# Four two-bank PSUM tiles become eight one-bank tiles, and every operation on PSUM takes 512 columns

## The chip, the cores and the metric

One core of one Trainium2 chip. The metric is the device time of one execution in microseconds; where several executions are shown, their median.

## The reference

Three layers over 4 sequences of 768 tokens, in fp32: a linear attention with a decaying state per head, a feed-forward block with a squared relu, and an RMS norm with a gated feed-forward block.

```python
# attention: 8 heads of 64
for t in range(S):
    state = gamma * state + einsum('bhd,bhe->bhde', k[:, :, t], v[:, :, t])
    y[:, :, t] = scale * einsum('bhd,bhde->bhe', q[:, :, t], state)
x = y as [3072, 512]
# first feed-forward, 512 -> 2048 -> 512
h = maximum(x @ w_in, 0);  x = (h * h) @ w_out
# second, 512 -> 1536 -> 512
xn = x / sqrt(mean(x * x) + 1e-6) * rms_g
g = xn @ w_gate;  val = xn @ w_val
out = (g * sigmoid(g) * val) @ w_out2
```

## The kernel before

**Precision.** Each fp32 operand is kept as a high and a low fp32r part (`split`: a cast on ScalarE, a subtraction on VectorE, line 90). A product is three matmuls of 512 columns: high by high, high by low, low by high (`mm3`, lines 173, 174 and 175). `proj` is the four contraction blocks of one output block: twelve matmuls.

**PSUM.** Four tiles, `pa`, `pb`, `ph` and `pr`, each [128, 2, 512] fp32 and so two banks of 2 KB per partition: all eight banks. They live for the whole kernel. A half of one is `ph[:, 0]` or `ph[:, 1]`; some operations read or write a whole tile, 1024 columns.

**Order.** The whole body stands under `manual_schedule`: on each engine the instructions run in the order in which the code issues them. The framework puts in the semaphore waits: an instruction that writes a tile waits for those that read it before, and one that reads waits for those that wrote.

**Stages.** Tokens go in blocks of 512 (six), chunks of 128 for the attention. The times are those of the profiled execution.

- 0 to 258 us: `block1` for blocks 0 and 1, a plain feed-forward, with the attention's chunks visited in between (`scores`, lines 613 to 624, with the mask's multiplication at line 623; `values`; `into_state`). Projections alternate between `ph[:, 0]` and `ph[:, 1]`; the output blocks collect in `pa` and `pb`. `norm1` copies these out.
- 258 to 397 us and 487 to 613 us: `in_phase` for a pair of blocks, 32 projections, again alternating between the two halves of `ph`. Behind each, ScalarE applies relu from PSUM (line 320) and squares in SBUF (line 321). In the second in-phase the weights come through a ring of seven SBUF units that DMA fills, and beside it the weights of the second feed-forward are converted and written back to HBM (`tick`: `magnitude` at line 138 on ScalarE, `convert` on VectorE, then a DMA).
- 397 to 487 us and 613 to 718 us: `out_phase`, the product with `w_out` for a pair of blocks, by a scheme of seven products (P2, P1, P5, P6, P7, P3, P4 in this order) in place of eight. Four units of twelve matmuls for each product; P2, P5 and P3 collect in `pr`, the others in `ph`, and P6, P7, P4 and P3 add to what stands there from the product before. At the end of a product, the tile is copied to SBUF (line 370 for P6, by halves, 372 for P2, P5 and P4) or added to an SBUF tile (line 376 through line 100).
- 718 to 1315 us: three sweeps, one for each pair of blocks, of six calls of `pair` (line 511): gate and value projections by the same seven products, twelve matmuls each, `pr` for P2, P5 and P3, `ph` for P1, P6, P7 and P4. ScalarE copies (525, 530, 535), VectorE adds (line 100), and `act2` makes the gated value: sigmoid on ScalarE (478), the gate's multiplication (480) and the value's (481) on VectorE, and a split. The last `act2` of a pair reads `ph` itself: 478 and 480 its first half, 481 its second. Between P1 and P5 and before P7 stand matmuls of the output product into `pa` and `pb`; what is left of it runs at the end of a sweep (`out2_late`), a block of 36 matmuls into alternating halves of `pr`, each copied out at line 508.

Of the kernel before, what the change touches and what calls it, by code (L numbers as in the profile page):

```python
# [51 lines left out]
def retention_then_two_mlps(  # L52
# [22 lines left out]
    pa, pb, ph, pr = (ps.tile([128, 2, TB], F32, name=n) for n in ("pa", "pb", "ph", "pr"))  # L75
# [23 lines left out]
    def plus(out_, a, b):  # L99
        nc.vector.tensor_tensor(out=out_, in0=a, in1=b, op=ALU.add)  # L100

# [75 lines left out]
    class Operand:  # L177
# [13 lines left out]
        def put(self, o, src, two_banks):  # L191
            if self.whole and not two_banks:
                split(self.t[0][0][:, :, o], self.t[1][0][:, :, o], src, nc.vector)
            elif self.whole:
                h, l = (t[0][:, :, o].rearrange("p (k a) i -> p k a i", k=2) for t in self.t)
                split(h, l, src, nc.vector)
            else:
                for k in range(2):
                    split(self.t[0][k][:, :, o], self.t[1][k][:, :, o], src[:, k], nc.vector)
# [22 lines left out]
    accs = [pa[:, 0], pa[:, 1], pb[:, 0], pb[:, 1]]  # L222
# [9 lines left out]
    def sums(tot):  # L232
        if due:
            tots, sqs = due.pop(0)
            tots.append(tot)
            for i, sq in enumerate(sqs):
                for h in range(2):
                    for c in range(2):
                        n = 2 * c + h
                        nc.tensor.matmul(  # L240
                            tot[c * D:(c + 1) * D, i, h * C:(h + 1) * C], ones, sq[:, n * C:(n + 1) * C],
                            start=True, stop=True,
                        )

    def rsqrt(js, sqs, last=False):
# [6 lines left out]
        nc.vector.tensor_scalar(m, tots[0], 1.0 / DM, EPS, op0=ALU.mult, op1=ALU.add)  # L252
# [13 lines left out]
    def norm1(j):  # L266
        y = [slot("y") for _ in range(2)]
        for i, (eng, src) in enumerate(((nc.scalar, pa), (nc.vector, pb))):
            copy(eng, y[i], src)
            nc.sync.dma_start(ys[j][:, 2 * i:2 * i + 2, :], y[i])  # L270
        yield
        yield
        for i in range(2):
            nc.scalar.activation(y[i], y[i], AF.Square)
            yield
        for a, b in ((y[0][:, 0], y[0][:, 1]), (y[1][:, 0], y[1][:, 1]), (y[0][:, 0], y[1][:, 0])):
            nc.gpsimd.tensor_tensor(out=a, in0=a, in1=b, op=ALU.add)
            yield
        yield
        yield from rsqrt([j], [y[0][:, 0]])  # L280
# [29 lines left out]
    def in_phase(xs, w_of, after, between):  # L310
        for f in range(NF1):
            q, r, i = f // 4, f % 4 // 2, f % 2
            w = w_of(f)
            for t in range(2):
                proj(w, xs[t], ph[:, t])
# [4 lines left out]
                nc.scalar.activation(a, ph[:, t], AF.Relu)  # L320
# [22 lines left out]
    def out_phase(s, pairs, ahead, y_tile, extra):  # L343
# [9 lines left out]
        for n in range(NOUT):  # L353
# [4 lines left out]
            for m in range(2):  # L358
                mc = slice(m * 128, (m + 1) * 128)
                for c in range(2):  # L360
                    mm3(
                        acc[:, m], u[:, c, 0, mc], u[:, c, 1, mc], xh[:, c], xl[:, c],
# [148 lines left out]
    def pair(n, first, second):  # L511
# [13 lines left out]
        nc.scalar.copy(p1, ph)  # L525
        plus(p1, pr, p1)
# [3 lines left out]
        nc.scalar.copy(p5, pr)  # L530
# [4 lines left out]
        nc.scalar.copy(p6, ph)  # L535
# [4 lines left out]
        plus(p5, ph, p5)  # L540
        act2(p5[:, 0], p5[:, 1], U2[f + 1])
        both(P3, pr, False)
        plus(p6, pr, p6)
        act2(p6[:, 0], p6[:, 1], U2[f])
        both(P4, ph, False)
        act2(ph[:, 0], ph[:, 1], u1[1])

    with tc.manual_schedule():
# [64 lines left out]
        def scores(c, banks, early=False):  # L613
# [3 lines left out]
            sc = banks.rearrange("p h (a i) -> p h a i", a=NP)  # L617
            P = slot("Pt").rearrange("p h (a i) -> p h a i", a=NP)
            for p in range(NP):
                for h, b in enumerate(heads):  # L620
                    nc.tensor.matmul(sc[:, h, p, :], k_[b, p, :], qq[b, p, :], start=True, stop=True)
            table = decays if early else tri_sb.unsqueeze(1).unsqueeze(1).to_broadcast([128, 2, NP, C])
            nc.vector.tensor_tensor(out=P, in0=sc, in1=table, op=ALU.mult)
            pt[c] = P

        def into_state(c):
# [3 lines left out]
            kv = pr[:, 1, 2 * C:].rearrange("p (a d) -> p a d", a=NP)  # L630
# [40 lines left out]

        def visit(c, next_banks, with_sums):
            kv = into_state(c)
            if with_sums:
                sums(pr[:, 0:1, 2 * C:])
            values(c, [pr[:, i, :2 * C].rearrange("p (a i) -> p a i", a=2) for i in range(2)])
# [3 lines left out]
        def after_visit(c, x, kv):  # L680
            x.put(columns_of(c), pr[:, :, :2 * C].rearrange("p k (a i) -> p k a i", a=2), True)
# [16 lines left out]
        warm = ph[:PQ, 0, :128]  # L698
# [14 lines left out]
        def early_values(c, bank):  # L713
            values(c, [bank.rearrange("p (a i) -> p a i", a=NP)])
            cur.put(columns_of(c), bank.rearrange("p (a i) -> p a i", a=NP), False)
# [6 lines left out]
        early_values(0, pr[:, 1])  # L722
# [4 lines left out]
        early_values(1, pr[:, 0])  # L727
        scores(3, pb, early=True)
        early_values(2, ph[:, 0])
        early_values(3, ph[:, 1])  # L730
# [39 lines left out]
        def block1(j, x, sink, visit_at, early, late):  # L770
            nonlocal prev, at_chunk
            first_at = 2 if j == 0 else None
            for f in range(NF1):
# [5 lines left out]
                proj(W[("i", f)], x, ph[:, f % 2])  # L779
                s, r = act1(ph[:, f % 2])  # L780
# [141 lines left out]
        while back:  # L922
            if due:
                sums(pa[:, 0:1, :2 * C])
# [29 lines left out]
        def between2(f, t):  # L954
            background()
            if (f, t) == (3, 0):
                sums(pa[:, :, :2 * C])
# [90 lines left out]
        for s in range(NS):  # L1048
# [7 lines left out]
            for p in range(NPR):  # L1056
                def first():
                    if s == 0:
                        split_wp()
                        load_wp(p + 2)  # L1060
                        if p == 0:
                            sums(pa[:, :, :2 * C])
# [25 lines left out]
            out2_late(0, pr[:, 0])  # L1088
            some(4)
            give(NF2 - 1, 1)  # L1090
            store2(2 * s + 1, 0, pr[:, 0])
            for c in range(1, CB):
                l = pr[:, c % 2]
# [74 lines left out]
```

## Time and profile before

| | us |
|---|---|
| three runs | 1326.19, 1320.39, 1319.2 |
| median | 1320.39 |
| profiled execution | 1317.13 |
| its span in the trace | 1315.3 |
| TensorE busy in it | 1179.9 (90%) |
| VectorE busy | 746.1 (57%) |
| ScalarE busy | 590.3 (45%) |

The busy time of TensorE is modelled: matmuls overlap, and the row of one is longer than its step to the next. The time that a stop costs is read from the starts.

### The profile page before, as it was taken

Reading aid. Unit: us, or ns where it says so; the run is one execution under the profiler, and the core shown is the slowest. Engines: PE = TensorE matmul, PEld = TensorE weight load, DVE = VectorE, ACT = ScalarE, POOL = GpSimd, SP = SyncE. Lnnn points to the kernel's source line nnn. Section 1 sums busy time; section 2 is a strip of 40 time slices with the busy share of each in tenths; the row PEclk is TensorE's granted clock in tenths of the full one; section 3 lists DMA queues with packets and bytes.
Section 4 is the critical chain, followed back from the end, with each engine's and each line's share of the span. In section 5 each row is a group of like instructions: output and inputs, shape, how many; then the busy total and the mean of one; then the engine's idle time right before and its main releaser. Section 6 shows DMA issues by size and latency. Waiting matters only on the chain.

```text
span 1315.3 us, 15650 instructions
## 1 busy us (share of the span) xinstructions
PE 1179.9 (90%) x6070; PEld 930.4 (71%) x6070; DVE 746.1 (57%) x990; ACT 590.3 (45%) x997; POOL 46.2 (4%) x39
## 2 busy tenths in 40 slices
PE   7999998888889898688887899999899999899998
PEld 5788887666667576456665677777677777777776
DVE  5775266523235645432666776776576775667740
ACT  5786435444343425444334445443344443444431
POOL 0000211121100000000000000000000000000000
PEclk9999999999999899899999899999999999999999
DMA  9642455665664378863451121122111122111001
GB/s 362 256 161 89 145 186 201 231 224 207 224 240 160 131 242 269 315 227 112 161 180 68 38 84 49 38 71 100 41 56 33 40 88 81 44 54 32 33 0 65
DMA packets 74211, 175.45 MB, mean 133 GB/s; under 512 B 7948, under 2 KB 20632, under 8 KB 73880
## 3 DMA queue, kind: packets, MB, share of 16 engines
q1 hardware_dynamic: 73560, 174.24, 38.2%
q8 instruction: 48, 0.79, 0.2%
q10 hardware_dynamic: 576, 0.20, 0.1%
q14 instruction: 27, 0.22, 0.1%
HBM read 129.31 MB, written 45.10 MB: 133 GB/s over the span
## 4 chain that ended last, share of the span: by engine, by line
PE 57%; DVE 20%; ACT 14%; issue 5%; DMA 4%; SPq 0%; ACTq 0%; DVEq 0%
PE ph L173 11%; PE ph L174 9%; PE ph L175 9%; PE pr L173 5%; PE pr L174 5%; PE pr L175 5%; DVE part L100 3%; DVE t L481 2%; ACT act L320 2%; DVE t L480 2%; DVE act L97 2%; DVE ring L90 2%; PE pa L173 2%; ACT o L93 2%; PE pa L174 2%
## 5 line engine op out<-in xcount | busy, mean ns | idle before, releaser
L173 PE MATMUL ph<-xop,ring 128*128 128x512 f32 x288 | 116.2, 404 | 25.5 <-DVE t L481 20.9
L173 PE MATMUL ph<-xh,w_i 128*128 128x512 f32 x256 | 104.1, 407 | 30.1 <-ACT act L320 21.6
L174 PE MATMUL ph<-xop,ring 128*128 128x512 f32 x288 | 114.6, 398 | 0.0
L175 PE MATMUL ph<-xop,ring 128*128 128x512 f32 x288 | 114.5, 398 | 0.0
L174 PE MATMUL ph<-xl,w_i 128*128 128x512 f32 x256 | 100.0, 391 | 0.0
L175 PE MATMUL ph<-xh,w_i 128*128 128x512 f32 x256 | 99.8, 390 | 0.0
L173 PE MATMUL pr<-xop,ring 128*128 128x512 f32 x216 | 86.4, 400 | 8.0 <-DVE part L100 6.6
L173 PEld LDWEIGHTS ph<-xop,ring 128*128 128x128 f32 x288 | 55.4, 192 | 43.4 <-DVE t L481 27.2
L174 PE MATMUL pr<-xop,ring 128*128 128x512 f32 x216 | 85.5, 396 | 0.0
L175 PE MATMUL pr<-xop,ring 128*128 128x512 f32 x216 | 85.5, 396 | 0.0
L173 PEld LDWEIGHTS ph<-xh,w_i 128*128 128x128 f32 x256 | 48.0, 187 | 52.5 <-ACT act L320 31.8
L320 ACT ACTIVATE act<-ph 128x512 f32<-128x512 f32 x64 | 38.1, 595 | 104.7 <-PE ph L175 104.7
L90 DVE TENSOR_TENSOR o<-act,o 128x1024 fp32r<-128x1024 f32 x38 | 45.9, 1223 | 62.6 <-ACT o L93 62.6
L173 PE MATMUL ph<-xh,ring 128*128 128x512 f32 x128 | 54.2, 424 | 27.8 <-ACT act L320 26.7
L90 DVE TENSOR_TENSOR ring<-q,ring 128x512 fp32r<-128x512 f32 x90 | 57.4, 686 | 30.6 <-ACT ring L93 30.6
L478 ACT ACTIVATE t<-part 128x512 f32<-128x512 f32 x54 | 34.1, 632 | 79.7 <-DVE part L100 79.7
L93 ACT CAST o<-act 128x1024 fp32r<-128x1024 f32 x38 | 39.1, 1047 | 63.5 <-DVE act L97 60.6
L175 PEld LDWEIGHTS ph<-xop,ring 128*128 128x128 f32 x288 | 55.5, 193 | 12.0
L174 PEld LDWEIGHTS ph<-xop,ring 128*128 128x128 f32 x288 | 55.4, 192 | 11.3
L100 DVE TENSOR_TENSOR part<-pr,part 128x1024 f32<-128x1024 f32 x37 | 45.2, 1220 | 26.7 <-ACT part L525 26.5
L173 PE MATMUL pr<-wp,u 128*128 128x512 f32 x132 | 52.3, 396 | 5.1 <-ACT o L508 5.1
L173 PEld LDWEIGHTS ph<-xh,ring 128*128 128x128 f32 x128 | 24.4, 190 | 45.3 <-ACT act L320 39.3
(230 smaller groups left out, 2785.9 us busy)
## 6 DMA issues: line engine op xcount, KB each, us to landing
ring<-uo SPq DMA_DIRECT2D x56, 512.0 KB, 3.3
q<-wq SPq DMA_DIRECT2D x72, 256.0 KB, 3.2
raw<-w1i SPq DMA_DIRECT2D x16, 512.0 KB, 7.4
raw<-w1o SPq DMA_DIRECT2D x16, 512.0 KB, 6.9
uo<-made SPq DMA_DIRECT2D x16, 512.0 KB, 2.9
wi<-w_i SPq DMA_DIRECT2D x16, 512.0 KB, 5.8
ring<-wi SPq DMA_DIRECT2D x16, 512.0 KB, 4.3
uo<-w_o SPq DMA_DIRECT2D x24, 256.0 KB, 5.1
```

What stands on the lines that cost most here:

```text
L90: eng.tensor_tensor(out=dst_l, in0=src, in1=dst_h.bitcast(F32), op=ALU.subtract)
L93: nc.scalar.copy(dst_h, src)
L97: nc.vector.tensor_tensor(out=out_, in0=a, in1=b, op=ALU.subtract)
L100: nc.vector.tensor_tensor(out=out_, in0=a, in1=b, op=ALU.add)
L173: nc.tensor.matmul(acc, ah, bh, start=start, stop=False, **more)
L174: nc.tensor.matmul(acc, ah, bl, start=False, stop=False, **more)
L175: nc.tensor.matmul(acc, al, bh, start=False, stop=stop, **more)
L320: nc.scalar.activation(a, ph[:, t], AF.Relu)
L478: nc.scalar.activation(t, g, AF.Sigmoid)
L480: nc.vector.tensor_tensor(out=t, in0=g, in1=t, op=ALU.mult)
L481: nc.vector.tensor_tensor(out=t, in0=v, in1=t, op=ALU.mult)
```

## The change

Each of `pa`, `pb`, `ph` and `pr` becomes a list of two [128, 512] tiles, one bank each. Whatever read or wrote a whole tile becomes two instructions of 512 columns, the first bank ahead of the second: the copies (`take`), the adds (`add`), the mask's multiplication in `scores`, the splits in `put`, the first step of `rsqrt`. In `norm1` each tile is copied by both engines, ScalarE its first bank and VectorE its second, in place of one engine for each tile. The rest changes only how a bank is named. VectorE's instructions become 100 more, ScalarE's 74; TensorE's stay as many as they were. The kernel after has other line numbers: its rows name the matmuls of `mm3` as lines 181 to 183 and the multiplications of `act2` as 482 and 483.

```diff
-    pa, pb, ph, pr = (ps.tile([128, 2, TB], F32, name=n) for n in ("pa", "pb", "ph", "pr"))
+    pa, pb, ph, pr = ([ps.tile([128, TB], F32, name=f"{n}{i}") for i in range(2)] for n in ("pa", "pb", "ph", "pr"))
...
+    def take(dst, acc):
+        for m in range(2):
+            nc.scalar.copy(dst[:, m], acc[m])
+
+    def add(dst, acc):
+        for m in range(2):
+            plus(dst[:, m], acc[m], dst[:, m])
...
-        nc.vector.tensor_scalar(m, tots[0], 1.0 / DM, EPS, op0=ALU.mult, op1=ALU.add)
+        for i in range(n):
+            nc.vector.tensor_scalar(m[:, i], tots[0][i], 1.0 / DM, EPS, op0=ALU.mult, op1=ALU.add)
...
-        for i, (eng, src) in enumerate(((nc.scalar, pa), (nc.vector, pb))):
-            copy(eng, y[i], src)
+        for i, src in enumerate((pa, pb)):
+            for m, eng in enumerate((nc.scalar, nc.vector)):
+                copy(eng, y[i][:, m], src[m])
...
             for t in range(2):
-                proj(w, xs[t], ph[:, t])
+                proj(w, xs[t], ph[t])
...
-                nc.scalar.activation(a, ph[:, t], AF.Relu)
+                nc.scalar.activation(a, ph[t], AF.Relu)
...
-                if k == P6:
-                    a = get(0, 1)
-                    for m in range(2):
-                        nc.scalar.copy(a[:, m], acc[:, m])
-                elif k in (P2, P5, P4):
-                    nc.scalar.copy(get(*{P2: (0, 0), P5: (1, 1), P4: (1, 0)}[k]), acc)
+                if k in (P2, P5, P6, P4):
+                    take(get(*{P2: (0, 0), P5: (1, 1), P6: (0, 1), P4: (1, 0)}[k]), acc)
                 else:
                     a = {P1: (0, 0), P7: (1, 1), P3: (0, 1)}[k]
-                    t = y[a[0]][a[1]]
-                    plus(t, acc, t)
+                    add(y[a[0]][a[1]], acc)
                     store(*a)
...
-                product(acc[:, m], k, m, start)
+                product(acc[m], k, m, start)
...
-        nc.scalar.copy(p1, ph)
-        plus(p1, pr, p1)
+        take(p1, ph)
+        add(p1, pr)
...
-        nc.scalar.copy(p5, pr)
+        take(p5, pr)
...
-        nc.scalar.copy(p6, ph)
+        take(p6, ph)
...
-        plus(p5, ph, p5)
+        add(p5, ph)
...
-        plus(p6, pr, p6)
+        add(p6, pr)
...
-        act2(ph[:, 0], ph[:, 1], u1[1])
+        act2(ph[0], ph[1], u1[1])
...
-            nc.vector.tensor_tensor(out=P, in0=sc, in1=table, op=ALU.mult)
+            for h in range(2):
+                table = decays[:, h] if early else tri_sb.unsqueeze(1).to_broadcast([128, NP, C])
+                nc.vector.tensor_tensor(out=P[:, h], in0=sc[h], in1=table, op=ALU.mult)
...
-            out2_late(0, pr[:, 0])
+            out2_late(0, pr[0])
...
-                l = pr[:, c % 2]
+                l = pr[c % 2]
```

Three places in the engines' order. In the names, a number behind a name counts tiles: `ring_3297` and `ring_3352` are the same unit of weights; `ph_153` and `ph_154` are the two banks of `ph` after the change, `pr_155` and `pr_156` those of `pr`. A wait names the engine or DMA queue whose semaphore it reads.

TensorE, second in-phase, two projections in a row; before:

```order
L173 MATMUL ph<-xh,ring_3297 128x512 [waits DMAHW3_49,Activation_49]
L174 MATMUL ph<-xl,ring_3297 128x512
L175 MATMUL ph<-xh,ring_3297 128x512
...
L173 MATMUL ph<-xh,ring_3297 128x512 [waits Activation_49]
L174 MATMUL ph<-xl,ring_3297 128x512
```

and after:

```order
L181 MATMUL ph_153<-xh,ring_3352 128x512 [waits DMAHW3_49,Activation_49]
L182 MATMUL ph_153<-xl,ring_3352 128x512
L183 MATMUL ph_153<-xh,ring_3352 128x512
...
L181 MATMUL ph_154<-xh,ring_3352 128x512 [waits Activation_49]
L182 MATMUL ph_154<-xl,ring_3352 128x512
```

Nothing moved. The wait for ScalarE stands at the same instructions; the tile that it protects is `ph` before, and one bank of it after.

TensorE, P1 of a pair in the sweeps, its first half and the start of its second; before:

```order
L173 MATMUL ph<-xop,ring_3297 128x512 [waits DVE_49]
L174 MATMUL ph<-xop,ring_3297 128x512
L175 MATMUL ph<-xop,ring_3297 128x512
L173 MATMUL ph<-xop,ring_3297 128x512
L174 MATMUL ph<-xop,ring_3297 128x512
L175 MATMUL ph<-xop,ring_3297 128x512
L173 MATMUL ph<-xop,ring_3297 128x512
```

and after:

```order
L181 MATMUL ph_153<-xop,ring_3352 128x512 [waits DVE_49]
L182 MATMUL ph_153<-xop,ring_3352 128x512
L183 MATMUL ph_153<-xop,ring_3352 128x512
L181 MATMUL ph_153<-xop,ring_3352 128x512
L182 MATMUL ph_153<-xop,ring_3352 128x512
L183 MATMUL ph_153<-xop,ring_3352 128x512
L181 MATMUL ph_154<-xop,ring_3352 128x512 [waits DVE_49]
```

One wait for VectorE has become two, one for each bank, six matmuls apart.

VectorE, the end of a pair: the adds of P7 and P3, the three gated values; before:

```order
L100 TENSOR_TENSOR part_4820<-ph,part_4820 128x1024 [waits PE_49]
L480 TENSOR_TENSOR t<-part_4820,t 128x512 [waits Activation_49]
L481 TENSOR_TENSOR t<-part_4820,t 128x512 [waits DVE_49]
L100 TENSOR_TENSOR part_4886<-pr,part_4886 128x1024 [waits PE_49]
L90 TENSOR_TENSOR u_5107<-t,u_5107 128x512 [waits Activation_49]
L480 TENSOR_TENSOR t<-part_4886,t 128x512 [waits Activation_49]
L481 TENSOR_TENSOR t<-part_4886,t 128x512 [waits DVE_49]
L90 TENSOR_TENSOR u_5107<-t,u_5107 128x512 [waits Activation_49]
L480 TENSOR_TENSOR t<-ph,t 128x512 [waits Activation_49]
L481 TENSOR_TENSOR t<-ph,t 128x512 [waits DVE_49]
```

and after:

```order
L100 TENSOR_TENSOR part_4885<-ph_153,part_4885 128x512 [waits PE_49]
L100 TENSOR_TENSOR part_4885<-ph_154,part_4885 128x512 [waits PE_49]
L482 TENSOR_TENSOR t<-part_4885,t 128x512 [waits Activation_49]
L483 TENSOR_TENSOR t<-part_4885,t 128x512 [waits DVE_49]
L100 TENSOR_TENSOR part_4952<-pr_155,part_4952 128x512 [waits PE_49]
L100 TENSOR_TENSOR part_4952<-pr_156,part_4952 128x512 [waits PE_49]
L90 TENSOR_TENSOR u_5176<-t,u_5176 128x512 [waits Activation_49]
L482 TENSOR_TENSOR t<-part_4952,t 128x512 [waits Activation_49]
L483 TENSOR_TENSOR t<-part_4952,t 128x512 [waits DVE_49]
L90 TENSOR_TENSOR u_5176<-t,u_5176 128x512 [waits Activation_49]
L482 TENSOR_TENSOR t<-ph_153,t 128x512 [waits Activation_49]
L483 TENSOR_TENSOR t<-ph_154,t 128x512 [waits DVE_49,PE_49]
```

Each add of two banks has become two instructions with a wait on TensorE of their own, and the last multiplication has a wait on TensorE for its bank.

## Rows read from the trace of the kernel before

**Rows 1.** What TensorE waited for, whole span: total us, times, longest us.

```profile
PE ph L173 <- ACT act L320: 48.3, 54, 6.7
PE ph L173 <- DVE t L481: 20.9, 14, 1.9
...
PE pr L173 <- DVE part L100: 6.6, 3, 2.4
PE pr L173 <- ACT o L508: 6.6, 9, 1.0
PE ph L173 <- DVE Pt L623: 5.2, 4, 2.6
...
PE ph L173 <- ACT y L370: 4.0, 1, 4.0
...
PE ph L173 <- ACT y L372: 1.1, 1, 1.1
```

**Rows 2.** The same view, the first in-phase alone (258 to 397 us).

```profile
PE ph L173 <- ACT act L320: 21.6, 24, 3.0
```

**Rows 3.** The same view, the second in-phase alone (486 to 613 us).

```profile
PE ph L173 <- ACT act L320: 26.7, 30, 6.7
```

**Rows 4.** Timeline, TensorE, second in-phase: start, duration, instruction, idle before and releaser.

```profile
502.51 0.50 PE L173 MATMUL ph<-xh,ring 128*128 128x512 f32 x1 [0.69 <-ACT act L320]
502.85 0.40 PE L174 MATMUL ph<-xl,ring 128*128 128x512 f32 x1
503.09 0.39 PE L175 MATMUL ph<-xh,ring 128*128 128x512 f32 x1
```

**Rows 5.** Windows: length, busy us of engines, granted clock, DMA share, GB/s.

```profile
258.00:397.00 139.00, 117.37 (x819) 87.67 (x817) 41.44 (x57) 60.52 (x110) 21.17 (x16) 1.00 0.63 220
490.00:580.00 90.00, 69.39 (x284) 50.02 (x282) 45.82 (x67) 47.26 (x75) 0.00 (x0) 0.96 0.82 285
530.00:540.00 10.00, 3.33 (x12) 2.42 (x11) 2.11 (x4) 2.46 (x4) 0.00 (x0) 0.73 0.93 365
580.00:613.00 33.00, 26.94 (x108) 19.77 (x109) 1.23 (x1) 11.91 (x19) 0.00 (x0) 1.00 0.33 112
```

**Rows 6.** Timeline, all engines, around TensorE's longest stop.

```profile
537.17 0.66 ACT L138 ACTIVATE f<-raw 128x512 f32<-128x512 f32 x1 [7.88 <-DMA wq<-f]
...
538.96 0.63 PE L174 MATMUL ph<-xl,ring 128*128 128x512 f32 x1
...
539.38 0.63 PE L175 MATMUL ph<-xh,ring 128*128 128x512 f32 x1
```

**Rows 7.** Groups by form: count, busy us, mean ns, idle before and releaser.

```profile
L100 DVE TENSOR_TENSOR part<-pr,part 128x1024 f32<-128x1024 f32 x37 | 45.2, 1220 | 26.7 <-ACT part L525 26.5 <-PE pr L175 0.2
...
L525 ACT COPY part<-ph 128x1024 f32<-128x1024 f32 x18 | 18.3, 1015 | 25.0 <-PE ph L175 25.0
...
L370 ACT COPY y<-ph 128x512 f32<-128x512 f32 x2 | 1.1, 584 | 0.0
```

**Rows 8.** Timeline, VectorE, a pair of the second sweep.

```profile
1015.41 1.29 DVE L90 TENSOR_TENSOR ring<-q,ring 128x512 fp32r<-128x512 f32 x2 [1.24 <-ACT ring L93]
...
1022.00 1.23 DVE L100 TENSOR_TENSOR part<-ph,part 128x1024 f32<-128x1024 f32 x1
1023.99 0.69 DVE L480 TENSOR_TENSOR t<-part,t 128x512 f32<-128x512 f32 x1 [0.76 <-ACT t L478]
...
1025.32 1.22 DVE L100 TENSOR_TENSOR part<-pr,part 128x1024 f32<-128x1024 f32 x1
...
1027.30 0.69 DVE L480 TENSOR_TENSOR t<-part,t 128x512 f32<-128x512 f32 x1 [0.16 <-ACT t L478]
...
1030.02 0.68 DVE L480 TENSOR_TENSOR t<-ph,t 128x512 f32<-128x512 f32 x1
1030.73 0.69 DVE L481 TENSOR_TENSOR t<-ph,t 128x512 f32<-128x512 f32 x1
```

**Rows 9.** Timeline, TensorE, P1 of the pair that follows.

```profile
1031.47 0.50 PE L173 MATMUL ph<-xop,ring 128*128 128x512 f32 x1 [1.35 <-DVE t L481]
```

More of the change, by code (lines that the diff above doesn't have):

```diff
@@ L189, in __getitem__, with put @@
             ]
[L191 to L195, printed above, removed]
+        def put(self, o, banks):
+            n = KC // len(banks)
+            for k, src in enumerate(banks):
+                a = slice(n * k, n * k + n) if self.whole else slice(0, n)
+                h, l = (t[0 if self.whole else k][:, a, o] for t in self.t)
                 split(h, l, src, nc.vector)
-            else:
-                for k in range(2):
-                    split(self.t[0][k][:, :, o], self.t[1][k][:, :, o], src[:, k], nc.vector)
     def proj(w, x, h):
@@ L616, in scores @@
             qq, k_, _, _ = chunk[c]
-            sc = banks.rearrange("p h (a i) -> p h a i", a=NP)
+            sc = [b.rearrange("p (a i) -> p a i", a=NP) for b in banks]
             P = slot("Pt").rearrange("p h (a i) -> p h a i", a=NP)
@@ L620, in scores @@
                 for h, b in enumerate(heads):
-                    nc.tensor.matmul(sc[:, h, p, :], k_[b, p, :], qq[b, p, :], start=True, stop=True)
-            table = decays if early else tri_sb.unsqueeze(1).unsqueeze(1).to_broadcast([128, 2, NP, C])
-            nc.vector.tensor_tensor(out=P, in0=sc, in1=table, op=ALU.mult)
+                    nc.tensor.matmul(sc[h][:, p, :], k_[b, p, :], qq[b, p, :], start=True, stop=True)
+            for h in range(2):
+                table = decays[:, h] if early else tri_sb.unsqueeze(1).to_broadcast([128, NP, C])
+                nc.vector.tensor_tensor(out=P[:, h], in0=sc[h], in1=table, op=ALU.mult)
             pt[c] = P
@@ L670, in columns_of, with halves @@
             return slice((c % B) * C, (c % B + 1) * C)
+        def halves():
+            return [b[:, :2 * C].rearrange("p (a i) -> p a i", a=2) for b in pr]
         def visit(c, next_banks, with_sums):
@@ L674, in visit @@
             if with_sums:
-                sums(pr[:, 0:1, 2 * C:])
-            values(c, [pr[:, i, :2 * C].rearrange("p (a i) -> p a i", a=2) for i in range(2)])
+                sums([pr[0][:, 2 * C:]])
+            values(c, halves())
             scores(c + 1, next_banks)
@@ L680, in after_visit @@
         def after_visit(c, x, kv):
-            x.put(columns_of(c), pr[:, :, :2 * C].rearrange("p k (a i) -> p k a i", a=2), True)
+            x.put(columns_of(c), halves())
             take_state(c, kv)
@@ L714, in early_values @@
             values(c, [bank.rearrange("p (a i) -> p a i", a=NP)])
-            cur.put(columns_of(c), bank.rearrange("p (a i) -> p a i", a=NP), False)
+            cur.put(columns_of(c), [bank.rearrange("p (a i) -> p a i", a=NP)])
         scores(0, pa, early=True)
@@ L956, in between2 @@
             if (f, t) == (3, 0):
-                sums(pa[:, :, :2 * C])
+                sums([b[:, :2 * C] for b in pa])
             if 1 <= f <= 11:
@@ L1061, in first @@
                         if p == 0:
-                            sums(pa[:, :, :2 * C])
+                            sums([b[:, :2 * C] for b in pa])
                             background()
```

26 lines of the change are left out of this document (13 added, 13 removed).

## The prediction

> **What bounds the kernel now.** I read the list of what TensorE waits for first: the matmuls are a fixed series, and whatever stops them lengthens the kernel unless something later was waiting anyway. Its largest entry is one kind of stop, 48.3 us in 54 waits of a projection for the relu of line 320; the next are 20.9 us in 14 waits for the second multiplication of line 481, and 6.6 us each for the adds of line 100 and the copies of line 508 [rows 1]. All are waits to write a PSUM tile that ScalarE or VectorE still reads. The same list by stage puts 21.6 us of the relu's in the first in-phase (258 to 397 us) [rows 2] and 26.7 us in the second (487 to 613 us) [rows 3].
>
> Then the timeline of one such stop, for its price. Matmuls start 0.23 us apart (502.85 and 503.09); behind the stop, which shows 0.69 us idle, the first one lasts 0.50 and the next starts 0.34 later [rows 4]. With 0.39 busy in a usual row against 0.23 from start to start, a stop costs its idle time, plus 0.16, plus 0.11: **idle + 0.27 us**. The reader should see that the stop comes although the projection writes the other half of ph than the one that relu reads: the wait belongs to the tile, not to the bank.
>
> Third, the windows, for what else is near its limit there. The DMA engines are 0.63 busy in the first in-phase, 0.82 in 490 to 580 us, and 0.93 in the ten microseconds in which TensorE stood longest [rows 5]. That stop, the 6.7 of the second in-phase [rows 3], began at ScalarE, which had stood 7.88 us for a transfer, and behind it matmuls start 0.42 us apart (538.96, 539.38), at a granted clock of 0.73 in that window: for part of it the clock was at the lower of its two levels, 1.2 GHz [rows 5, 6].
>
> **The change, part by part.** No matmul, transfer or arithmetic is added or moved. Each engine keeps its order. Two things differ: 174 instructions over two banks become two each (100 on VectorE, 74 on ScalarE), and waits attach to a bank.
>
> *What a split costs.* A 128x1024 add takes 1220 ns, and a 128x512 instruction on VectorE 0.69 us [rows 7, 8]; a 1024 copy takes 1015 ns and a 512 one 584 [rows 7]. Two queued 512s on VectorE span 1.29 us together (1015.41) [rows 8] against 1.22. So a split costs 0.06 to 0.07 us where the two queue behind each other, and at most 2 x 0.69 - 1.22 = 0.16 or 2 x 0.584 - 1.015 = 0.15 where nothing overlaps; 174 x 0.16 = 28 us if all stood on the path. I take the low end, and charge it inside the chains below, since adjacent instructions of one engine overlap in every row of this kind. On the side of the gain, the reader who waits for both halves gets the first half sooner, and the part that must follow the last matmul shrinks from 1.22 to 0.69, or 1.02 to 0.58.
>
> A rule speaks against this. The Trainium skill, Advanced Engine Details and Errata (TRN2 Errata, The Read-Write Bubble), says that memory accesses are not pipelined from one instruction to the next and advises large tiles, even several PSUM banks in one instruction. Its page Perfetto Trace Analysis (Optimizing Scalar/DVE Operations) puts the overhead on PSUM at about 125 ns for VectorE and 51 for ScalarE: an estimate of 100 x 0.125 + 74 x 0.051 = 16 us of engine time, which would be 16 us of span only if no split were hidden. The same section adds that instructions which are not saturating their engine but hold up others may gain by being broken up.
>
> *In-phase 1.* A projection (12 matmuls, 2.72 us) now waits for the relu of the one before the last. The relu has a whole projection to finish in, and every stop seen but one is under 2.72 us. That one, 3.0 us [rows 2], keeps 0.3. Available: 21.6 + 24 x 0.27 = 28.1; I take **27.5**. What could be late next is DMA: 0.63 x 139 us of transfer work in 111.5 us is a share of 0.79, below the 0.93 seen.
>
> *In-phase 2.* Available are 26.7 + 30 x 0.27 = 34.8 us. But from 490 to 580 the transfers weigh: 0.82 x 90 = 74 us of DMA work, which at the highest share seen, 0.93, needs 79 us. So of that stretch 11 us can go, against 23 if TensorE set its length (284 matmuls x 0.23 = 65 us and some waits), and nothing if 0.82 is all that DMA does on a mean. Behind 580 us nine projections follow (108 matmuls) at a DMA share of 0.33 [rows 5], each with the usual stop of 0.69 + 0.27 = 0.96: 8.6. I take 11 + 8.6 = **19.6**, ends 8.6 and 32.
>
> *Out phases.* The wait for line 372 (1.1 + 0.27) goes, because bank 0 is copied while bank 1 is still accumulated: 1.4. The 4.0 us for line 370 [rows 1] stays in large part, since ScalarE was late there for reasons of its own queue; I take 1.0, and 1.0 more for half of the matmuls at the lower clock behind it. **3.4**, ends 0 and 7.5.
>
> *Pairs.* P1 of the next pair waits 1.35 us for line 481, which reads ph's second half; with 0.27 that is 1.62 [rows 8, 9]. With banks, P1's first six matmuls wait only for line 480, and the second six, 1.36 us later, for line 481. Line 480 started 0.71 earlier (1030.02 against 1030.73). To lose the stop wholly it must come another 0.91 earlier. It does so by the chain ahead of it. An add started at 1022.00 and line 480 behind it at 1023.99: the sigmoid between them waited for the add of both banks and needs only that of bank 0, a gain of 1.22 - 0.69 = 0.53. The next add at 1025.32 leads to line 480 at 1027.30, 1.98 later [rows 8]; here two adds and a subtraction stand ahead on VectorE, three steps of 0.60 (1.29 - 0.69) or 1.81 with what is between them, a gain of 0.17. A copy whose first bank is read 1.36 us ahead of the last matmul leaves 1.02 - 0.58 = 0.4 to its followers. Together 0.53 + 0.17 + 0.4 = 1.1 against 0.91: it goes with only **0.2 us to spare**. I take it whole for the ten pairs of sweeps 2 and 3 (16.2). The four of sweep 1 stand for 20.9 - 13.5 = 7.4 of idle; with 4 x 0.27, less 0.3 each that I leave, 7.3. Behind two of these four, the longest of them (1.9), fifteen matmuls in all start 0.42 apart as in rows 6, 0.2 us lost on each: 3.0, and five more, 1.0, behind one of the waits of 2.4 below [rows 1]. The nine waits for the copy of line 508 go, since the banks alternate: 6.6 + 9 x 0.27 = 9.0. The three waits for line 100 (6.6 in all, the longest 2.4) [rows 1], each a two-bank copy and a two-bank add in series, become a one-bank copy and add that start six matmuls sooner: the two longest go, 2 x (2.36 + 0.27) = 5.2, and of the third, at the start of the sweeps, 1.2 of its 1.8: 6.4. Sum 16.2 + 7.3 + 4.0 + 9.0 + 6.4 = **42.9**, ends 19 (no stop at line 481 gained) and 46.
>
> *Start.* Four waits for line 623 [rows 1], each 0.53 sooner: **2.1**.
>
> Sum: 27.5 + 19.6 + 3.4 + 42.9 + 2.1 = 95.5. The profiled execution took 1317.13 us, so 1221.6; the median of the runs was 3.3 above that execution, which gives 1224.9, say **1225 us**.
>
> **The rivals.** *DMA is the bound of the second in-phase already.* For it: the long stop there comes from a transfer. Against: 0.93 was reached. If the share cannot rise above its mean of 0.82, the 11 us are lost: 1236.
>
> *Line 480 comes no sooner.* VectorE's chain takes the place of the wait: 0.2 us of margin is thin, and each split adds 0.06 on it. If 14 stops keep 1.0 us each, 1239; with the first rival, 1250.
>
> *The change doesn't release what it says.* Then a wait is still for both halves, and the time stays at about 1320. Against it: the rows of the new order name the bank in each tile, and the last multiplication has a wait on TensorE of its own for its bank.
>
> *Slower.* Every split pays its full 0.16 us on the path, in chains where VectorE or ScalarE is the last: 28 us, and the chains were long before; 1348 if no wait is given back. It decides as soon as the waits given back are under 28 us; the first in-phase alone holds that, where no instruction at all is split. The page of the Trainium skill (Perfetto Trace Analysis, Optimizing Scalar/DVE Operations) would make it 16 us, 1336.
>
> **How the numbers follow.** The forecast 0.58 (1207 to 1231: all of 32 in the second in-phase, or the out phases and pairs short by a few); DMA 0.14; VectorE's chain, alone or with DMA, 0.20; nothing released 0.04; slower 0.04. The range 1205 to 1248 takes in the first three and the cost ends named, up to both rivals together less 2 us. A measurement can tell 0.5% from no change, 6.6 us: faster 0.93, same 0.03, slower 0.04.
>
> **What would show it.** In the profile after: no wait of a projection for the relu in 258 to 370 us, and a stage some 27 us shorter; in the second in-phase some waits for the relu left, each behind a ScalarE instruction that stood for a transfer, and a DMA share near 0.9; the lines that were 480 and 481 start sooner than before, and P1 shows no wait, or one under 0.3 us; the banks of line 508 alternate without a stop; two 512 adds 0.60 us apart. Wrong would make it: stops of 1 us left at P1 (the chain), waits for the relu with no transfer behind them (not released), or pairs that last over 26 us each.

## The result, and the profile after

The kernel after takes 1218.95 us (median of 4 runs, 1216.87 to 1221.62) against 1319.8 before: a ratio of 0.9235, 95% interval 0.919 to 0.9279. The profiled execution took 1216.87 us, 100.3 us less than the one of before; its span is 1215.0.

The engines' busy time (part 1 of the page): TensorE is at 95% in place of 90%, with less busy time in all: before, more rows were long (behind a stop, or at the lower clock), and a row behind a stop doesn't overlap with the one ahead of it.

```profile
PE 1155.6 (95%) x6070; PEld 934.2 (77%) x6070; DVE 743.0 (61%) x1090; ACT 593.7 (49%) x1071; POOL 44.4 (4%) x39
```

What TensorE waited for, whole span, as in [rows 1] (us in total, times, longest):

```profile
PE ph L181 <- ACT act L327: 10.0, 2, 8.3
PE ph L182 <- DVE o L90: 8.1, 14, 1.0
PE ph L181 <- DVE part L100: 5.8, 1, 5.8
PE ph L181 <- DVE Pt L626: 5.0, 4, 2.3
...
PE ph L181 <- ACT y L104: 3.5, 1, 3.5
...
PE pr L181 <- DVE part L100: 1.3, 1, 1.3
...
PE ph L181 <- DVE t L482: 0.2, 1, 0.2
```

The relu, line 320 before and 327 now, fell from 48.3 us in 54 waits to 10.0 in two. Line 481 (now 483) is gone from the list, and the gate's multiplication ahead of it, now 482, holds P1 once, for 0.2 us. The copies of line 508 are gone. The adds of line 100, for which a product in `pr` waited, are 1.3 in place of 6.6. The mask's multiplication, 5.2 before at line 623, is 5.0 at line 626. One wait has grown: near the start of the sweeps `ph` waits 5.8 us for line 100, where before it was 4.5.

The windows of both in-phases and of the sweeps (length, busy us of TensorE, its weight loads, VectorE, ScalarE and GpSimd, granted clock, DMA share, GB/s), the counterpart of [rows 5]:

```profile
260.00:371.00 111.00, 110.38 (x819) 89.46 (x817) 40.05 (x70) 60.58 (x118) 20.41 (x16) 1.00 0.79 275
460.00:534.00 74.00, 63.98 (x284) 51.81 (x283) 45.57 (x68) 46.66 (x74) 0.00 (x0) 0.95 0.95 348
500.00:510.00 10.00, 7.23 (x25) 5.86 (x26) 5.06 (x9) 6.80 (x11) 0.00 (x0) 0.69 0.97 364
...
716.00:1186.00 470.00, 469.92 (x2066) 386.80 (x2065) 337.81 (x509) 216.85 (x375) 0.00 (x0) 1.00 0.17 56
```

TensorE stands still for 0.6 us in the first in-phase and for 0.1 in the 470 us of the sweeps from 716 on. In the second in-phase the DMA engines are at 0.95 for 74 us.

Where the 100 us went, by aligning the two traces at the same matmul at each stage's border:

| stage | before, us | after, us | gained | predicted |
|---|---|---|---|---|
| 0 to 257.5 of before | 257.6 | 259.5 | -1.9 | 2.1 |
| in-phase 1 | 141.5 | 111.8 | 29.7 | 27.5 |
| out phase 1 | 88.7 | 86.4 | 2.3 | 3.4, both out phases |
| in-phase 2 | 126.0 | 101.3 | 24.7 | 19.6 |
| out phase 2 | 104.5 | 103.7 | 0.8 | in the 3.4 above |
| sweeps | 593.2 | 548.5 | 44.7 | 42.9 |

### The profile page after: what moved, and what is told of

It is laid out like the page before. It is cut to its first block, busy times and chain, and to the rows that moved or that the text cites. A ratio compares the mean times of both kernels' runs of the same rounds, so it can differ in the third digit from the quotient of the medians.

```text
span 1215.0 us, 15870 instructions
## 1 busy us (share of the span) xinstructions
PE 1155.6 (95%) x6070; PEld 934.2 (77%) x6070; DVE 743.0 (61%) x1090; ACT 593.7 (49%) x1071; POOL 44.4 (4%) x39
## 4 chain that ended last, share of the span: by engine, by line
PE 77%; DVE 10%; ACT 7%; issue 3%; DMA 3%; SPq 0%; ACTq 0%; DVEq 0%
PE ph L181 13%; PE ph L182 12%; PE ph L183 12%; PE pr L181 7%; PE pr L182 7%; PE pr L183 7%; DVE act L97 2%; PE pa L181 2%; PE pa L182 2%; PE pa L183 2%; PE pb L181 2%; PE pb L183 2%; PE pb L182 2%; ACT o L93 2%; DMA wq<-f 1%
## 5 line engine op out<-in xcount | busy, mean ns | idle before, releaser
L181 PE MATMUL ph<-xop,ring 128*128 128x512 f32 x288 | 113.5, 394 | 6.0 <-DVE part L100 5.8
L182 PE MATMUL ph<-xop,ring 128*128 128x512 f32 x288 | 112.6, 391 | 0.0
L183 PE MATMUL ph<-xop,ring 128*128 128x512 f32 x288 | 112.6, 391 | 0.0
L183 PE MATMUL ph<-xh,w_i 128*128 128x512 f32 x256 | 100.3, 392 | 0.0
L181 PE MATMUL pr<-xop,ring 128*128 128x512 f32 x216 | 85.0, 393 | 1.4 <-DVE part L100 1.3
L182 PE MATMUL pr<-xop,ring 128*128 128x512 f32 x216 | 84.8, 393 | 0.0
L183 PE MATMUL pr<-xop,ring 128*128 128x512 f32 x216 | 84.6, 392 | 0.0
L181 PEld LDWEIGHTS ph<-xop,ring 128*128 128x128 f32 x288 | 54.4, 189 | 20.1 <-DVE part L100 6.2
L183 PEld LDWEIGHTS ph<-xop,ring 128*128 128x128 f32 x288 | 54.4, 189 | 11.4
L182 PEld LDWEIGHTS ph<-xop,ring 128*128 128x128 f32 x288 | 54.4, 189 | 11.1
L181 PEld LDWEIGHTS ph<-xh,w_i 128*128 128x128 f32 x256 | 48.4, 189 | 18.4 <-DVE Pt L626 6.7
L181 PE MATMUL ph<-xh,ring 128*128 128x512 f32 x128 | 51.0, 398 | 10.0 <-ACT act L327 10.0
L146 ACT ACTIVATE f<-raw 128x512 f32<-128x512 f32 x68 | 45.4, 669 | 29.9 <-DMA wq<-f 16.0
L183 PEld LDWEIGHTS ph<-xh,w_i 128*128 128x128 f32 x256 | 48.4, 189 | 10.7 <-DVE w_i L90 0.4
L182 PEld LDWEIGHTS ph<-xl,w_i 128*128 128x128 f32 x256 | 48.5, 189 | 10.3 <-DVE xl L90 0.5
```

Source lines behind the costliest of these rows:

```text
L146: nc.scalar.activation(sizes[i], loads[i].bitcast(F32)[:, :, 1], AF.Prelu, scale=REBIAS, alpha=NEGATIVE)
L181: nc.tensor.matmul(acc, ah, bh, start=start, stop=False, **more)
L182: nc.tensor.matmul(acc, ah, bl, start=False, stop=False, **more)
L183: nc.tensor.matmul(acc, al, bh, start=False, stop=stop, **more)
```

## The experiments

The first four keep one part of the change, or do one part alone; e1 in an expectation is the first of them. Gains of a stage are read, as in the table, by aligning the traces at the same matmul. The kernel of before was run beside each series of experiments, with medians of 1320.7 to 1322.0 us against the 1319.8 above, so totals that differ by 2 us between series say little.

### The splits without the banks

```diff
-    pa, pb, ph, pr = ([ps.tile([128, TB], F32, name=f"{n}{i}") for i in range(2)] for n in ("pa", "pb", "ph", "pr"))
+    def pair_of(n):
+        t = ps.tile([128, 2, TB], F32, name=n)
+        return [t[:, i] for i in range(2)]
+    pa, pb, ph, pr = (pair_of(n) for n in ("pa", "pb", "ph", "pr"))
```

> The four tiles are two banks each again, but every operation on PSUM takes 512 columns as in the kernel after: the splits without the freed waits. Theory (the gain comes from waits by bank, a split costs 0.06 to 0.07 us where it is queued): the time of the kernel before plus 0 to 8 us, 1318 to 1328 us, with the relu's wait still near 48 us in 54 waits. Rival (the gain comes from the shorter operations): well under 1300 us. Rival (each split pays 0.16 us on the path): 1348 us.

Measured: 1315.38 us, ratio 0.9953 (0.9935 to 0.9972). Half of a percent faster, 3 us below the range that was expected, so neither 28 us slower nor more than 6 of the 100 us. The list of waits (in this kernel line 333 is the relu, 489 the value's multiplication, 516 the copy out, 106 the add):

```profile
PE ph L187 <- ACT act L333: 51.6, 54, 7.3
PE ph L187 <- DVE t L489: 11.2, 14, 1.2
...
PE pr L187 <- ACT o L516: 5.8, 8, 0.7
```

The 54 waits for the relu stay, and so does the copy out. What falls is P1's wait, from 20.9 to 11.2 us in the same 14 places. One of its rows in the second sweep (start, duration, instruction, idle before it), and from the next pair the adds of P7 and the sigmoid behind the first of them:

```profile
1006.20 0.50 PE L187 MATMUL ph<-xop,ring 128*128 128x512 f32 x1 [0.64 <-DVE t L489]
...
1022.89 1.29 DVE L106 TENSOR_TENSOR part<-ph,part 128x512 f32<-128x512 f32 x2
...
1023.68 0.64 ACT L486 ACTIVATE t<-part 128x512 f32<-128x512 f32 x1 [2.05 <-DVE part L106]
```

1.35 has become 0.64: 0.71 us a pair from the splits alone. The sigmoid of `p5`'s first half starts at 1023.68, while the second of the two adds still runs: in SBUF it waits only for the half that it reads. That is the size of the 0.53 + 0.17 = 0.70 of the prediction's chain. The sweeps gain 14.0 us by alignment, and in-phase 1 loses 7.0, in-phase 2 1.7: in the first, ScalarE's wait for the low part of the visits' operand, which VectorE works out from `pr`, is 17.0 us in 8 places against 7.4 in 4. In the kernel with the same splits and `pr` in one-bank tiles (the second of the next section) this wait is not in the list and that stage takes 142.6 us, 1.1 more than before: so it is the two-bank `pr` through which the halves hold each other up there.

### One tile at a time

In `pair_of`, one-bank tiles for the one name and views of a two-bank tile for the others:

```diff
     def pair_of(n):
+        if n == "ph":
+            return [ps.tile([128, TB], F32, name=f"{n}{i}") for i in range(2)]
         t = ps.tile([128, 2, TB], F32, name=n)
```

> Only ph becomes two one-bank tiles; pa, pb and pr keep two banks, operations take 512 columns. Theory: the relu's waits and those of P1 for line 481 go, 29.7 and 24.7 us in the in-phases and most of the 24 us of P1, while the 9.0 us for line 508 and 5 us for line 100, both in pr, stay: 1232 to 1242 us. If P1's chain needs the early add of P3 in pr too, its stops come back in part: up to 1250 us.

Measured: 1236.62 us, ratio 0.9364 (0.9332 to 0.9396).

```profile
PE ph L187 <- ACT act L333: 10.4, 3, 8.4
...
PE pr L187 <- ACT o L516: 5.8, 8, 0.7
...
PE pr L187 <- DVE part L106: 4.7, 3, 1.9
```

The relu's waits are where they are after the change, in-phase 1 gains 28.3 us and in-phase 2 24.1. The waits in `pr` stay: 5.8 us in 8 for the copy out and 4.7 in 3 for the adds, against 1.3 in one after the change. With 0.27 each that is 12 of the 18 us that separate this kernel from the whole change; by alignment 14 of the 18 are in the sweeps.

The same with `pr` in the place of `ph`:

> Only pr becomes two one-bank tiles, the complement: theory, the waits for line 508 (9.0 us) and line 100 (about 5) go, and the splits' cost of e1 is paid: 1300 to 1312 us; the gains of this and of ph alone add up to that of the whole change within some 8 us. If pa and pb matter, the sum falls short by more.

Measured: 1293.91 us, ratio 0.9798 (0.9771 to 0.9825), some 6 us better than the lower end of what was expected, since I had charged the splits a cost that they do not have on balance.

```profile
PE ph L187 <- ACT act L333: 48.8, 54, 6.7
...
PE pr L187 <- DVE part L106: 4.1, 3, 1.4
```

48.8 us of relu stay, and the copy out is gone. Of the adds' waits 4.1 us are left, and with `ph` alone 4.7, against 1.3 after the whole change: these need both tiles. Gains against the kernel of before: 84.7 for `ph`, 27.4 for `pr`; both hold the 5.9 of the splits, so 106 together against 101 for the whole. They add up within 5 us, which leaves nothing for `pa` and `pb`; a kernel with `ph` and `pr` alone wasn't run.

### The freed wait alone, in one stage

```diff
-                proj(w, xs[t], ph[:, t])
+                proj(w, xs[t], halves[t])
...
-                nc.scalar.activation(a, ph[:, t], AF.Relu)
+                nc.scalar.activation(a, halves[t], AF.Relu)
...
-        in_phase(xs2, w_of2, after2, between2)
+        in_phase(xs2, w_of2, after2, between2, [ph[:, 0], pr[:, 0]])
```

> The kernel before, with one difference: in the second in-phase the projections alternate between the first half of ph and the first half of pr, two tiles, in place of the two halves of ph. No split, no other tile. Theory (the stop is a wait for a tile): that stage loses 23 to 26 us and nothing else changes, 1294 to 1298 us. Rival (the gain in that stage needs something else of the change): 1320 us.

Measured: 1297.88 us, ratio 0.9824 (0.9789 to 0.9858). The stage is 22.8 us shorter by alignment, with no instruction split and no tile changed. Its list of waits in that stage:

```profile
PE pr L173 <- ACT act L320: 9.0, 2, 8.3
PE ph L173 <- ACT act L320: 1.7, 1, 1.7
```

Thirty waits have become three, and one of 8.3 us is new. The kernel after has that one too, and of the same length. The third is the out phase's first write to `pr`, 0.7 us. So the stop behind the relu is the wait for a tile, and the long stop that is left doesn't come from the two halves being one tile.

### What is left in the second in-phase

In the kernel after, ScalarE's queue around the longest stop:

```profile
501.57 0.66 ACT L146 ACTIVATE f<-raw 128x512 f32<-128x512 f32 x1 [10.51 <-DMA wq<-f]
...
502.77 0.29 PEld L181 LDWEIGHTS ph<-xh,ring 128*128 128x128 f32 x1 [8.75 <-ACT act L327]
```

The conversion of line 146 stood 10.5 us for a store of an earlier one, and the relu stands behind it on ScalarE. Four kernels ask why.

```diff
-        if i < len(stream):
+        if i < len(stream) and not 7 * NQ <= i < 7 * NQ + NF1:
             nc.sync.dma_start(ring[i % 7].bitcast(F32), stream[i])
```

> The kernel after without the sixteen 512 KB loads of the ring in the second in-phase: its projections use what stands in the ring, so that this part of the result is not computed. Theory (after the change DMA is the bound of that stage): the stops of 8.3 and 1.7 us there and the slow clock behind them go, the stage falls from 101 to 89 to 92 us, 1206 to 1210 us in all. Rival (a shortage of buffers, not of transfer time): within 3 us of the kernel after, 1219.

Measured: 1214.14 us, ratio 0.9192 (0.917 to 0.9215), between the theory and its rival. The stage takes 98.9 us, and not the 89 to 92 that were expected. The windows say why (columns as above):

```profile
475.00:490.00 15.00, 15.00 (x79) 12.15 (x78) 11.23 (x16) 9.10 (x16) 0.00 (x0) 1.00 0.62 212
490.00:500.00 10.00, 3.84 (x17) 2.91 (x16) 0.84 (x3) 1.51 (x4) 0.00 (x0) 0.93 0.98 363
510.00:534.00 24.00, 23.54 (x104) 19.18 (x103) 17.10 (x25) 17.28 (x27) 0.00 (x0) 1.00 0.76 240
```

On a mean the transfers have room, 0.62 and 0.76 of the DMA engines' time on both sides, and the stop of 6.2 us is there all the same, in a stretch of ten microseconds at 0.98. Over the 74 us from 460 to 534 the share fell from 0.95 to 0.82, and the stage gained 2.4 us. That the sum of the transfers was the bound, as the prediction had it, falls; what is left to explain is the stretch of ten microseconds.

> The same omission in the kernel before (that part of the result is not computed either). Theory (there the relu's waits are the bound, and DMA only in one stop): at most the stop of 6.7 us and the slow clock behind it go, 1311 to 1316 us. If DMA had set that stage before already, 10 us or more: under 1310.

Measured: 1318.7 us, ratio 0.9984 (0.9965 to 1.0003); the stage gains 1.0 us, less than expected. Its longest stop is 5.2 us, in the place of the 6.7. The kernel of before is not bound by the sum of its transfers either.

```diff
-        cf = rctx.enter_context(tc.tile_pool(name="cf", bufs=3))
+        cf = rctx.enter_context(tc.tile_pool(name="cf", bufs=4))
```

> The kernel after with four buffers in place of three for the converted weights, whose store ScalarE waits for in the second in-phase (16.0 us in 6 waits). If transfer time is the bound there (share 0.95), the wait moves to another place and the time stays, 1216 to 1221 us. Rival (the number of buffers): the stops of 8.3 and 1.7 us shrink and 5 to 11 us are gained, 1208 to 1214 us.

Measured: 1216.1 us, ratio 0.9206 (0.9175 to 0.9237). What ScalarE waits for changes its name, from the store to the load of raw weights, and keeps its length:

```profile
ACT f L146 <- DMA raw<-w2v: 10.9, 2, 10.0
```

So neither buffers nor the mean share. What SyncE issues just ahead of the stop, in the kernel after:

```profile
488.22 0.90 SPq L985 DMA_DIRECT2D yn<-ys  x2
489.17 1.11 SPq L393 DMA_DIRECT2D rr<-rrs  x2
```

Two loads of 1 MB (`yn`) and two broadcasts (`rr`), and the conversions' stores and loads are issued behind them. The load of raw weights issued at 487.26, ahead of the four, landed after 3.8 us; the one issued at 490.81, behind them, after 11.9. That gave the next kernel: no conversion at the two visits behind these loads.

```diff
-            if 1 <= f <= 11:
+            if 1 <= f <= 13 and f not in (5, 6):
                 tick()
-            elif f == 12 and t == 0:
+            elif f == 14 and t == 0:
```

> The kernel after, with the weight conversions of the second in-phase at other visits: none at f = 5 and 6, behind the two 1 MB loads of yn issued at the end of f = 4, and two more at f = 12 and 13, with the opening of the late tiles at f = 14 in place of 12. The same work and transfers. Theory (a burst of transfers ahead of the raw weights holds ScalarE, and relu stands behind it): the stops of 8.3 and 1.7 us and the slow clock behind them go, the stage falls from 101 to 89 to 93 us, 1207 to 1212 us in all. Rival (the stage's whole transfer time is the bound): the stop comes at another place, 1216 us or more.

Measured: 1210.0 us (1208.6 to 1218.15), ratio 0.9146 (0.9096 to 0.9196); its interval touches that of the kernel after, and the profiled execution was the slowest of the five, already 2.8 us behind the kernel after at 260 us. Its stage gains only 1.6 us. The stop is 5.1 us in place of 8.3, and ScalarE stands there for something else:

```profile
ACT xop L93 <- DVE yn L400: 9.9, 3, 7.7
ACT f L146 <- DMA wq<-f: 8.2, 6, 4.0
```

Line 93 is the cast of `yn`, scaled on VectorE by line 400, which waited 13.5 us for the broadcast:

```profile
504.08 1.42 DVE L400 SCALAR_TENSOR_TENSOR yn<-yn,g_sb,rr 128x512 f32<-128x512 f32 x2 [13.53 <-DMA rr<-rrs]
```

The longest stop is no longer the conversions' but the normalization's, and in both kernels what is waited for was issued with or just behind the two loads. So the stop came at another place, as the rival had it, and this run does not decide between the two; what speaks against the rival's reason is the kernel without the ring's loads. That the burst of `yn` and `rr` is the cause is read from the traces: no run takes it away or moves it, and a kernel that also delays the normalization wasn't tried. What moving the conversions is worth stays open too: the median says 9 us, the trace 2.

### The margin at the end of a pair

```diff
         add(p6, pr)
+        for _ in range(2):
+            nc.vector.tensor_tensor(out=p6[:, 1], in0=p6[:, 1], in1=p6[:, 1], op=ALU.max)
```

> The kernel after with two more 128x512 VectorE instructions (0.60 us each in the queue, they change no value) in every pair between the add of P3 and the next multiplication, on the chain to line 482. The trace of the kernel after shows line 482 done 0.45 us ahead of P1; then 1.2 - 0.45 + 0.27 = 1.0 us comes back at each of 15 P1s: 1234 us. With the 0.2 us of the prediction 19 us, 1238. Rival (VectorE has more room than that): 1219 to 1222.

Measured: 1235.21 us, ratio 0.9364 (0.9332 to 0.9396), 16.3 above the kernel after; by alignment the sweeps lose 19.5.

```profile
PE ph L181 <- DVE t L482: 16.6, 15, 1.6
```

```profile
927.52 1.28 DVE L100 TENSOR_TENSOR part<-pr,part 128x512 f32<-128x512 f32 x2
928.84 1.42 DVE L547 TENSOR_TENSOR part<-part 128x512 f32<-128x512 f32 x2
930.17 0.69 DVE L90 TENSOR_TENSOR u<-t,u 128x512 fp32r<-128x512 f32 x1
...
934.22 0.50 PE L181 MATMUL ph<-xop,ring 128*128 128x512 f32 x1 [0.85 <-DVE t L482]
```

The two instructions put 1.45 us into the queue, and not 1.2: line 90 starts 2.65 us behind the add here and 1.20 behind it in the kernel after (919.51 and 920.71, shown with the pair in the part on the prediction). The stop is back at every one of the 15 places. In sweeps 2 and 3 a pair in the middle of a sweep, from P1 to P1, lasts 25.63 us in place of 24.48, so 1.15 of the 1.45 came back and 0.3 were covered; in the first sweep it lasts 26.2 in place of 24.8, and nothing was covered. The pairs of sweeps 2 and 3 after the change are bound by TensorE, with a third of a microsecond to spare on VectorE.

### Two further splits

The out phases still show the chain of subtraction, cast and low part, 1024 columns each, at line 90 (8.1 us in the list above, and more in `pr`). The same remedy as in the change, in SBUF:

```diff
-        if k == P5:
-            sub(x00, x01, x00)
+        c2 = [slice(0, 1), slice(1, 2)]
+        for c in c2:
+            if k == P5:
+                sub(x00[:, c], x01[:, c], x00[:, c])
...
-        split(*prepared[n], {P2: x10, P1: x00, P5: x00, P6: x00, P7: x01, P3: x11, P4: x10}[k], nc.vector)
+        for c in c2:
+            split(h[:, c], l[:, c], x[:, c], nc.vector)
```

> The kernel after, with the operands of the out phases prepared in halves of 512 columns as well: two subtractions, two casts, two low parts in place of one each of 1024, all in SBUF. Theory (in the second out phase the chain of subtraction, cast and low part, 3.5 us a unit against 2.72 of matmuls, is on the path, and halves overlap on the two engines): the waits for line 90 there, 10.5 us in 17, and part of the 4.2 for line 93 go with 0.27 each, 10 to 17 us in all, 1202 to 1209 us. Rival (more instructions on the path than they hide): 1219 to 1224 us.

Measured: 1193.83 us, ratio 0.9024 (0.8983 to 0.9065), 8 us beyond what was expected. Out phase 2 gains 13.8 us against the kernel after, as expected; out phase 1 9.5, which I had not counted. There the wait of 3.5 us at the copy of line 104 is nearly gone, with 13 matmuls at the lower clock behind it, and line 90 is 1.3 in place of 8.1 (the list, over the whole span):

```profile
PE ph L182 <- DVE o L90: 1.3, 3, 0.9
...
PE ph L181 <- ACT y L104: 0.3, 1, 0.3
```

ScalarE had come late to that copy because a cast of 1024 columns stood ahead of it, which itself had waited for a subtraction of 1024 columns (line 97). In the kernel after:

```profile
420.78 1.04 ACT L93 CAST oh<-act 128x1024 fp32r<-128x1024 f32 x1 [2.50 <-DVE act L97]
421.73 1.06 ACT L104 COPY y<-ph 128x512 f32<-128x512 f32 x2
```

```diff
-            for h in range(2):
+            for h in (1, 0):
                 table = decays[:, h] if early else tri_sb.unsqueeze(1).to_broadcast([128, NP, C])
```

> The kernel after, with the two mask multiplications of a chunk in the other order, second bank first. Theory (the projection behind a visit writes the second bank, whose reader comes last of the two, so the split gained nothing there): the four waits for this line, 5.0 us, fall by 0.5 to 0.6 each to about 2.8, 1216 to 1218 us, less than the runs scatter; the list of waits decides. Rival (it waits for both): 5.0 us stays.

Measured: 1214.47 us, ratio 0.9186 (0.9141 to 0.9231).

```profile
PE ph L181 <- DVE Pt L626: 3.4, 2, 1.7
```

Four waits, 5.0 us, are two, 3.4: two of 0.28 us are gone, and two of 2.2 are 1.7. So all four were for the second of the two banks; less is saved than the 2.2 expected because the short two had only 0.28 to give. The total differs from the kernel after by no more than the runs scatter.

> The three edits before this together on the kernel after: theory, their gains add, since they lie in three stages: 1190 to 1200 us. If one gives time back to another (the out phase earlier, with its loads closer to the conversions), up to 1206.

Measured: 1187.77 us (1187.61 to 1188.33), ratio 0.898 (0.894 to 0.9021): 31 us below the kernel after, and a little below the expected 1190. By the trace 21.7 us of it are in the two out phases, 4.3 in in-phase 2, 2.6 ahead of in-phase 1.

## Why the prediction was right

The forecast was 1225 us, the time 1218.95, in the range and in the case given 0.58. By its own steps:

- **In-phase 1**: 27.5, measured 29.7. No wait for the relu is left from 260 to 371 us, the one of 3.0 included, which I had left 0.3 of. The DMA share is 0.79, as worked out. The price of a stop, idle + 0.27, holds: 28.1 of the 29.7 are its sum.
- **In-phase 2**: 19.6, measured 24.7, within the ends 8.6 and 32. This is the term whose reasoning failed while its size nearly held, by luck. I took the stage's summed transfer time as a bound, at a share of 0.93. After the change the same 284 matmuls ran at 0.95 for 74 us, and the experiment without the ring's loads shows that even this was no bound. What held TensorE lies in some ten microseconds, which no mean over 90 us tells; in the trace of before the 0.93 of the ten microseconds around the longest stop [rows 5] was that stretch, with the same two loads issued at 524.69, and I read it as a ceiling. The remaining loss is one stop of 8.3 us, one of 1.7, and the slow clock behind the first.
- **Out phases**: 3.4, measured 3.1 (2.3 and 0.8), in part by luck. The wait for line 372 went, as the 1.4 had it; at line 370's copy 0.5 us went and not 1.0, and nothing of the clock's 1.0 (12 matmuls at the lower level behind it, 11 before); the 0.8 of out phase 2 had no term. For the 4.0 us of line 370 the prediction's reason, ScalarE's own queue, is what the operands in halves showed: with them it is 0.3.
- **Pairs**: 42.9, measured 44.7. P1's stop went; its chain was shortened by 0.71 by the splits alone where the prediction had 0.70, and the margin of 0.2 us measures as 0.3 in sweeps 2 and 3 and as none in sweep 1, where a pair lasts 0.3 us longer than in the others, the 0.3 that the prediction left there. The rival in which VectorE's chain takes the place of the wait was that near: 1.45 us more on it brought back 16 us. The end of a pair in the trace after shows it (VectorE's rows, and P1's start):

```profile
919.51 1.28 DVE L100 TENSOR_TENSOR part<-pr,part 128x512 f32<-128x512 f32 x2
920.71 0.68 DVE L90 TENSOR_TENSOR u<-t,u 128x512 fp32r<-128x512 f32 x1
921.31 0.68 DVE L482 TENSOR_TENSOR t<-part,t 128x512 f32<-128x512 f32 x1
...
924.01 0.68 DVE L482 TENSOR_TENSOR t<-ph,t 128x512 f32<-128x512 f32 x1
924.80 0.69 DVE L483 TENSOR_TENSOR t<-ph,t 128x512 f32<-128x512 f32 x1
```

```profile
925.20 0.39 PE L181 MATMUL ph<-xop,ring 128*128 128x512 f32 x1
```

Line 482 ends at 924.69, P1 starts at 925.20 with no idle time; before, line 481 ended at 1031.42 and P1 started at 1031.47 [rows 8, 9]. The last matmul ahead of that P1 was

```profile
1029.74 0.39 PE L175 MATMUL pr<-xop,ring 128*128 128x512 f32 x1
```

and without a stop P1 would have started at 1029.97. Line 480 started 0.05 behind that before; now, as line 482, it starts 1.19 ahead of P1: 1.24 sooner, where the prediction had 1.1. Two queued adds take 1.28 us where one took 1.22.

- **The start**: 2.1, measured -1.9; this step was wrong, though small. Of the loss, 1.7 us lie in the first 30 us, which the change touches little, and two kernels that are word for word the same there as the one of before were 0.9 and 2.6 us later than it at that point: scatter. But the four waits for the mask's multiplication, 5.2 before and 5.0 after, did not fall by 0.53 each. The projection behind a visit writes the second bank, which is also multiplied second, and two queued multiplications end 0.06 us later than the undivided one. The swapped order shows it. What I left out was which of the two banks the waiting matmul writes.
- **The rivals.** Slower by the splits: on two-bank tiles they cost 8.7 us in the in-phases and gained 14.0 in the sweeps, 0.5% faster in all. The Trainium skill, Advanced Engine Details and Errata (TRN2 Errata, The Read-Write Bubble), advises larger tiles; here two queued halves cost 0.06 us more on VectorE, and what they start early is worth more. The Trainium skill, Perfetto Trace Analysis (Optimizing Scalar/DVE Operations), ties larger operations to a saturated engine, and says that breaking up instructions which hold up other engines may get work done sooner where the engine isn't saturated. The trace agrees: VectorE was busy for 61% of the span, ScalarE for 49%. DMA as the bound would have given 1236, and nothing released 1320: neither.

## What to carry to other kernels

Where one engine fills a buffer that others drain, count dependences in the unit in which the framework tracks them: halves of one tile wait for each other, two tiles don't, and alternating between two tiles gave one stage's gain without splitting anything. A split that costs 0.06 us where it queues paid where its first half freed someone, in SBUF as in PSUM, but not where both halves stayed in one tile that two engines read; look for the chain that is longer than the matmuls which it feeds. And a mean DMA share of 0.95 was no bound by itself: look for what is queued in front of the one transfer that an in-order engine waits for.

## What I had not expected of the hardware

The same stop, with the same idle time, was followed by either clock. In out phase 1 TensorE stood 3.52 us for the copy of line 104. In the kernel after the matmuls behind it start 0.43 us apart; the granted clock of 422 to 427 us is 0.50, the lower of the two levels:

```profile
422.36 0.80 PE L181 MATMUL ph<-oh,ring 128*128 128x512 f32 x1 [3.52 <-ACT y L104]
422.95 0.63 PE L182 MATMUL ph<-ol,ring 128*128 128x512 f32 x1
423.38 0.63 PE L183 MATMUL ph<-oh,ring 128*128 128x512 f32 x1
```

In the kernel with two more VectorE instructions, which is the same up to there, they start 0.23 us apart, at a granted clock of 1.00 from 420 to 425 us:

```profile
420.71 0.50 PE L181 MATMUL ph<-oh,ring 128*128 128x512 f32 x1 [3.52 <-ACT y L104]
421.05 0.39 PE L182 MATMUL ph<-ol,ring 128*128 128x512 f32 x1
421.28 0.39 PE L183 MATMUL ph<-oh,ring 128*128 128x512 f32 x1
```

That stage took 2.5 us less for it. Of four more of these kernels with the same stop of 3.51 to 3.53 us, two show twelve such slow matmuls behind it, one seven, and the one with the conversions at other visits none. So a forecast of what the clock gives back behind a stop of this length is good to no better than those microseconds; what decides it in these runs stays open.
